# Q and K loaded three tokens to a partition and turned by two identity products of 64 columns, instead of one token to a partition and one transpose of 128 columns

## The chip, the cores and the metric

One core of one Trainium2 chip runs the whole program. A core has a matrix engine (TensorE, PE in the rows, with its weight loads as PEld), a vector engine (DVE), a scalar engine (ACT), GpSimd (POOL) and SyncE (SP), which here issues the DMAs. The metric is the device time of one execution in microseconds (us), smaller is better.

## The reference, cut to what matters

The program chains an attention, a mixture of experts and a gated MLP. Only the first is touched:

```
B, H, S, D = 2, 8, 576, 64
q_d, k_d, v_d = mean of q, k, v over groups of 4 tokens
out_up    = repeat(softmax(q_d k_d^T / 8) v_d, 4)              # coarse, all to all
scores    = q k^T / 8, kept only where |i - j| < 4             # local window
out_local = softmax(scores) v
x = (out_up + out_local) as (1152, 512)
x = sum over 8 experts of P[:, e] * (relu(x @ w1[e]) @ w2[e])  # P from a gate, 8 rounds of scaling
h = x @ w_in;  out = (h * tanh(softplus(h))) @ w_out
```

## The kernel before

The attention works on one pair of heads at a time: 2 batches of 4 pairs give the pairs j = 0 to 7. For every pair Q and K have to lie with the channel on the partition (64 channels of one head above 64 of the other) and the 576 tokens along the free axis, since both score products contract over the channel.

- `load_qk` (tokens LQ and LK of the order) loads one of Q or K of a pair into a tile `qk` of 96 partitions by 12 rows of 64 channels: one DMA for each head, 96 partitions by 6 rows of 64 floats (256 bytes). Token 96u + p lies on partition p. There are 32 such DMAs of 144 KB. All input loads are issued by SP in one queue; four `qk` tiles exist, so a load waits until an older tile has been turned.
- `TP` (TP j.n.i, n = 0 for Q and 1 for K, i for the half of the tokens) turns 288 tokens: three transposes on PE by the identity, each from 96 tokens by 128 channels of both heads to 128 by 96, side by side in one PSUM tile (`at` or `aty`). 32 TPs in all.
- `TQ` and `TK` copy these 288 columns to `qt` or `kt` in SBUF (ACT for most, DVE for some; Q is scaled on the way). After them come `SQ`/`SK` (sums over 4 tokens for the coarse part, mostly POOL), `QL` (L795, the local scores, 16 small products a part, three parts a pair), `QD` (L805, the coarse scores), the softmaxes, `AV` and `AD` (L919, L928, the products with V), `XF` and finally `XH`/`XL` (L948, L951), which write the pair's rows of x as a high and a low half.

The order of all this is written out by hand in a string, ORDER; every engine takes its instructions strictly in that order. Mixed into it are fillers (FL, L1316: products on a constant tile that keep PE occupied), the loads (LD) and scaling of the first expert's weights, and from the token M0.0 on the first expert's products (`G1.products`, L1021), which need x of all four pairs of batch 0. The pairs of batch 1 go on between these products. After the attention PE has the experts' products (L1145, L1176) and then the MLP's.

Of the kernel before, what the change touches and what calls it, by code (L numbers as in the profile page):

```python
# [10 lines left out]
F32 = mybir.dt.float32  # L11
# [10 lines left out]
def attn_moe_moe2_kernel(ctx: ExitStack, tc: tile.TileContext, q, k, v, w_gate, w1, w2, w_in, w_out, out):  # L22
    nc = tc.nc
    B, H, S, D = q.shape
# [17 lines left out]
    QSC = 0.125 / 16.0  # L42
# [524 lines left out]
    ident = const.tile([128, 128], F32, name="ident")  # L567
# [59 lines left out]
    def tensor_engine(eng):  # L627
        return nc.gpsimd if eng == "G" else nc.vector
# [8 lines left out]
    def copy_on(eng, out, in_, scale=None):  # L637
        if eng == "A":
            nc.scalar.activation(out=out, in_=in_, func=AF.Copy, **({} if scale is None else dict(scale=scale)))
        elif scale is None:  # L640
            tensor_engine(eng).tensor_copy(out=out, in_=in_)
        else:
            nc.vector.tensor_scalar(out=out, in0=in_, scalar1=scale, scalar2=None, op0=ALU.mult)
# [5 lines left out]
    class Attention:  # L649
# [4 lines left out]

        def load_qk(self, src, j):

            t = self.p["qk"].tile([96, 12, D], F32, tag="qk", name="qk")
            for h in range(2):
                nc.sync.dma_start(out=t.rearrange("p (u h) d -> p u h d", h=2)[:, :, h],
                                  in_=src[self.b, 2 * j + h].rearrange("(u p) d -> p u d", p=96))  # L660
            return t

        def new_vw(self, j):
# [87 lines left out]
        def TP(self, j, n, i):  # L751

            t = self.st["qk"[n], j]
            ps = at_y() if self.b == 0 and i else self.at()
            for u in range(3):
                nc.tensor.transpose(ps[:, 96 * u:96 * u + 96], t[:, 6 * i + 2 * u:6 * i + 2 * u + 2].rearrange("p u d -> p (u d)"),
                                    ident[0:96, 0:96])
            self.st["T", j, n, i] = ps

        def TQ(self, j, i, eng):  # L760
            copy_on(eng, keep["qt"][j % 2][:, 288 * i:288 + 288 * i], self.st.pop(("T", j, 0, i))[:, 0:288], QSC)

        def TK(self, j, i, eng):
            copy_on(eng, keep["kt"][j % 2][:, 3 + 288 * i:291 + 288 * i], self.st.pop(("T", j, 1, i))[:, 0:288])

        def SQ(self, j, eng):
            self.pool_sum(keep["qd"][j % 2], keep["qt"][j % 2][:, 0:S], eng)
# [526 lines left out]
    with tc.manual_schedule():  # L1294
# [15 lines left out]
        def at_y():  # L1310
            return mm_pools[1][0].tile([128, 512], F32, tag=mm_pools[1][1], name="aty")
# [6 lines left out]
        def at2_tile():  # L1318
            return at2_p.tile([128, 2, 512], F32, tag="att", name="att")

        keep = {n: [pools["keep"].tile(sh, F32, name=f"{n}{i}") for i in range(2)]
                for n, sh in (("qt", [128, S + 8]), ("kt", [128, S + 8]), ("qd", [128, SD]), ("kd", [128, SD]),
                              ("ad", [HM, 2, 2, G, 32]))}
# [57 lines left out]
        def new_h():  # L1381
            return [hp.tile([128, 2, NT], F16, tag="h", name="h") for _ in range(FT)]
# [3 lines left out]
        h = new_h()  # L1386
# [85 lines left out]
        for e in range(1, E):  # L1472
            h = new_h()
# [385 lines left out]
        n = [0]  # L1859
# [27 lines left out]
        for c in range(NC2):  # L1887
            n = [0]
# [49 lines left out]
```

## Time and profile before

| | us |
|---|---|
| median of 3 runs | 968.1 (967.49 to 970.75) |
| the profiled execution, its own time | 969.7 |
| its span, first to last instruction | 967.7 |
| PE busy, share of the span | 949.1, 98% |
| PE products and weight loads | 8504 and 8504 |
| DVE busy | 720.6, 74% |
| ACT busy | 570.5, 59% |
| DMA packets under 512 bytes | 36812 of 97707 |

Busy time says that an engine held an instruction, not that it ran at its peak; neighbouring products overlap in it. The attention of batch 0 fills the first 53 us, that of batch 1 is spread over the next 60 us or so. Matmuls on 32-bit data stand twice in a row's count, a transpose once.

### The profile page before, as it was taken

How to read it: one execution, taken by the hardware profiler on the slowest of the kernel's cores; microseconds unless marked ns; L12 is line 12 of the kernel's file. 1: busy time of each engine (PE TensorE's matmuls, PEld its weight loads, DVE VectorE, ACT ScalarE, POOL GpSimd, SP SyncE). 2: the span in 40 equal slices, each digit the busy share in tenths (PEclk: the TensorE clock that was granted, in tenths of full speed). 3: DMA queues.
4: the chain of work that ended last, by engine and by line, in shares of the span. 5: the costliest groups of instructions: out<-in, count | busy, mean ns of one | idle time of the engine just before them, and what ended most of it. 6: DMA issues, size and time to landing. Idle time of an engine off the chain costs nothing.

```text
span 967.7 us, 20951 instructions
## 1 busy us (share of the span) xinstructions
PE 949.1 (98%) x8504; PEld 651.8 (67%) x8504; DVE 720.6 (74%) x1507; ACT 570.5 (59%) x1162; POOL 62.5 (6%) x116
## 2 busy tenths in 40 slices
PE   5999999999999999999999999999999999999998
PEld 4776674774576467547745764674477577999997
DVE  5887589589678968876796789588766468877731
ACT  4667364675577368646745874685465265666731
POOL 5524200000000000000000000000000000000000
PEclk9999999999999999999999999999999999999999
DMA  9962202021531443063215315141402756766770
GB/s 210 172 150 102 91 11 87 1 80 63 180 131 33 138 152 102 21 208 118 67 60 174 131 39 186 60 143 33 158 1 95 303 191 207 268 208 211 234 271 33
DMA packets 97707, 123.91 MB, mean 128 GB/s; under 512 B 36812, under 2 KB 72012, under 8 KB 96588
## 3 DMA queue, kind: packets, MB, share of 16 engines
q1 hardware_dynamic: 97612, 122.59, 40.4%
q8 instruction: 66, 1.08, 0.5%
q14 instruction: 29, 0.24, 0.1%
HBM read 104.48 MB, written 18.09 MB: 127 GB/s over the span
## 4 chain that ended last, share of the span: by engine, by line
PE 68%; DVE 7%; ACT 2%; DMA 1%; issue 1%; POOL 0%; SPq 0%; ACTq 0%; DVEq 0%; POOLq 0%
PE mm L1145 25%; PE mm L1176 24%; PE mm L1652 9%; PE n L1786 9%; DVE wal L356 1%; DVE acc L1209 1%; DVE raw L360 1%; DVE h L1120 1%; DVE wx L356 1%; DMA raw<-in_moe_w_dram 1%; DVE w L438 1%; DVE w L436 1%; DMA scri<-st 0%; ACT junk L267 0%; DVE st L472 0%
## 5 line engine op out<-in xcount | busy, mean ns | idle before, releaser
L1176 PE MATMUL mm<-wbh,h 128*128 128x512 f16 x1152 | 352.1, 379 | 0.0
L1176 PEld LDWEIGHTS <-h 128*128 128x128 f16 x1728 | 167.8, 98 | 191.9 <-issue 0.4
L1176 PE MATMUL mm<-wbl,h 128*128 128x512 f16 x576 | 218.3, 379 | 0.0
L1145 PE MATMUL mm<-x,wah 128*128 128x288 f16 x672 | 128.2, 286 | 1.5 <-ACT wbh L243 0.8
L1111 DVE SCALAR_TENSOR_TENSOR r<-mm,s 128x288 f32<-128x288 f32 x168 | 76.0, 455 | 71.1 <-PE mm L1145 53.0
L1145 PEld LDWEIGHTS <-wx 128*128 128x128 f16 x1008 | 98.6, 98 | 26.8 <-issue 2.0
L1145 PEld LDWEIGHTS <-wah 128*128 128x128 f16 x896 | 87.7, 98 | 27.8 <-issue 2.0
L1107 ACT ACTIVATE s<-mm 128x288 f32<-128x288 f32 x168 | 66.9, 408 | 58.9 <-PE mm L1145 58.5
L1145 PE MATMUL mm<-xt,wx 128*128 128x288 f16 x672 | 96.4, 286 | 1.3 <-DVE r L1111 1.2
L1652 PEld LDWEIGHTS <-win 128*128 128x128 f16 x1536 | 92.0, 98 | 6.4
L1145 PE MATMUL mm<-x,wal 128*128 128x288 f16 x336 | 96.1, 286 | 0.0
L1120 DVE SCALAR_TENSOR_TENSOR h<-r,h 128x576 f16<-128x576 f32 x112 | 81.2, 750 | 3.0 <-ACT h L1119 3.0
L1119 ACT ACTIVATE h<-r 128x576 f16<-128x576 f32 x112 | 74.1, 676 | 2.1 <-DVE r L1111 2.0
L445 ACT ACTIVATE junk<-w 128x512 bf16<-128x512 f32 x32 | 20.1, 627 | 73.4 <-DVE w L438 66.3
L1659 ACT ACTIVATE s<-mm 128x128 f32<-128x128 f32 x96 | 26.7, 278 | 53.3 <-PE mm L1652 51.4
L1652 PE MATMUL mm<-xc,win 128*128 128x128 f16 x864 | 55.7, 219 | 0.0
L267 ACT ACTIVATE junk<-raw 128x1024 bf16<-128x1024 f32 x52 | 54.6, 1049 | 1.4 <-DMA raw<-in_moe_w_dram 1.0
L98 POOL PARTITION_ALL_REDUCE ma<-m x25 | 12.3, 494 | 648.8 <-DVE m L273 311.5
L1209 DVE SCALAR_TENSOR_TENSOR acc<-mm,pc,acc 128x512 f32<-128x512 f32 x63 | 46.7, 745 | 9.6 <-PE mm L1176 9.6
L1145 PEld LDWEIGHTS <-wal 128*128 128x128 f16 x448 | 43.8, 98 | 11.0
L1145 PE MATMUL mm<-x,wx 128*128 128x288 f16 x336 | 50.3, 286 | 0.0
L1021 PE MATMUL mm<-x,wah 128*128 128x288 f16 x256 | 47.7, 286 | 0.0
(287 smaller groups left out, 1519.6 us busy)
## 6 DMA issues: line engine op xcount, KB each, us to landing
raw<-in_moe_w_dram SPq DMA_DIRECT2D x44, 512.0 KB, 5.4
win<-scri SPq DMA_DIRECT2D x40, 512.0 KB, 5.0
win<-scri SPq DMA_DIRECT2D x40, 384.0 KB, 3.5
raw<-in_moe_w_dram SPq DMA_DIRECT2D x10, 1024.0 KB, 6.2
f<-in_moe_w_in_dram SPq DMA_DIRECT2D x16, 512.0 KB, 3.9
f<-in_moe_w_out_dram SPq DMA_DIRECT2D x16, 512.0 KB, 3.7
scr<-st SPq DMA_DIRECT2D x32, 256.0 KB, 2.3
scri<-st SPq DMA_DIRECT2D x56, 128.0 KB, 1.8
```

The lines of the kernel that those rows point to most:

```text
L267: nc.scalar.activation(out=junk, in_=r[:, c * 1024:(c + 1) * 1024], func=AF.Square, accum_out=mx[:, 2 * i + c:2 * i + c + 1])
L1021: nc.tensor.matmul(self.ps, lhsT=wt[:, ws], rhs=x[:, xi, kk, o:o + CH], start=(n == 0), stop=(n == 3 * KT - 1))
L1107: nc.scalar.activation(out=t, in_=ps, func=AF.Copy, scale=HSC)
L1111: nc.vector.scalar_tensor_tensor(out=out, in0=ps, scalar=HSC, in1=r, op0=ALU.mult, op1=ALU.add)
L1119: lows.append((n + 3, lambda: nc.scalar.activation(out=hi, in_=r, func=AF.Relu)))
L1120: lows.append((n + 6, lambda: nc.vector.scalar_tensor_tensor(out=lo, in0=r, scalar=0.0, in1=hi, op0=ALU.max, op1=ALU.subtract)))
L1145: nc.tensor.matmul(ps, lhsT=w.part(wi, a)[:, c:c + 128], rhs=factor(b, bn, xi, i), start=(not before and k == 0), stop=(k == 5), skip_grou ...
L1176: nc.tensor.matmul(ps, lhsT=h[ft][:, hi, t * 128:(t + 1) * 128], rhs=wt[:, ws], start=(ft == 0 and n == 0), stop=(ft == FT - 1 and n == 2))
L1209: nc.vector.scalar_tensor_tensor(out=a, in0=ps, scalar=pc[:, t:t + 1], in1=a, op0=ALU.mult, op1=ALU.add)
L1652: nc.tensor.matmul(self.bank(bank), lhsT=self.win[i][:, n, wi, kk * 128:(kk + 1) * 128], rhs=self.x[:, xi, xn, kk * 128:(kk + 1) * 128], s ...
L1659: nc.scalar.activation(out=t, in_=self.ps[:, 0], func=AF.Copy)
L1786: nc.tensor.matmul(ps, lhsT=gt(c, f)[:, gi, a, :], rhs=wout[b][:, wi, f, :], start=(k == f == n == 0), stop=(k == len(terms) - 1 and f == ...
```

## The change

Q and K are loaded with three consecutive tokens on a partition: token 288i + 3p + u lies on partition p, so a DMA moves 96 partitions by 2 halves by 192 floats (768 bytes). The tile has the head outside, so the 128 channels of both heads no longer lie side by side; a TP is six products with the identity on the right, 96 tokens by 64 channels each, for u = 0, 1, 2 and for both heads, with the head's half of the PE columns and of the PSUM partitions. PSUM then holds the tokens in the order (u, p), and the copies TQ and TK read it as (p, u), that is with a step of 96 columns, and write `qt` and `kt` in the order of the tokens as before. The line numbers behind the new helper move by 5.

```diff
         def load_qk(self, src, j):
-            t = self.p["qk"].tile([96, 12, D], F32, tag="qk", name="qk")
+            t = self.p["qk"].tile([96, 2, 2, 3 * D], F32, tag="qk", name="qk")
             for h in range(2):
-                nc.sync.dma_start(out=t.rearrange("p (u h) d -> p u h d", h=2)[:, :, h],
-                                  in_=src[self.b, 2 * j + h].rearrange("(u p) d -> p u d", p=96))
+                nc.sync.dma_start(out=t[:, h], in_=src[self.b, 2 * j + h].rearrange("(i p u) d -> p i (u d)", i=2, u=3))
             return t
...
             for u in range(3):
-                nc.tensor.transpose(ps[:, 96 * u:96 * u + 96], t[:, 6 * i + 2 * u:6 * i + 2 * u + 2].rearrange("p u d -> p (u d)"),
-                                    ident[0:96, 0:96])
+                for h in range(2):
+                    nc.tensor.matmul(ps[D * h:D * h + D, 96 * u:96 * u + 96], lhsT=t[:, h, i, D * u:D * u + D],
+                                     rhs=ident[0:96, 0:96], start=True, stop=True, tile_position=(0, D * h))
             self.st["T", j, n, i] = ps
+        def thirds(self, j, n, i, to):
+            copy = self.st.pop(("T", j, n, i))[:, 0:288].rearrange("c (u p) -> c p u", u=3)
+            return to[:, 288 * i:288 * i + 288].rearrange("c (p u) -> c p u", u=3), copy
         def TQ(self, j, i, eng):
-            copy_on(eng, keep["qt"][j % 2][:, 288 * i:288 + 288 * i], self.st.pop(("T", j, 0, i))[:, 0:288], QSC)
+            copy_on(eng, *self.thirds(j, 0, i, keep["qt"][j % 2]), QSC)
         def TK(self, j, i, eng):
-            copy_on(eng, keep["kt"][j % 2][:, 3 + 288 * i:291 + 288 * i], self.st.pop(("T", j, 1, i))[:, 0:288])
+            copy_on(eng, *self.thirds(j, 1, i, keep["kt"][j % 2][:, 3:3 + S]))
```

No instruction changes its place; the rows of every engine stand in the same order as before. On PE, at the start of the program before the change (the TPs of pair 0, then two fillers):

```order
L756 MATMUL at<-ident,qk 128x96 x3
L1316 LDWEIGHTS warm
L1316 MATMUL fill<-warm 128x512
L756 MATMUL aty<-ident,qk 128x96 x6
L756 MATMUL at<-ident,qk 128x96 x3
L1316 LDWEIGHTS warm
```

And the same place of the change:

```order
L756 MATMUL at<-ident,qk 64x96 x6
L1321 LDWEIGHTS warm
L1321 MATMUL fill<-warm 128x512
L756 MATMUL aty<-ident,qk 64x96 x12
L756 MATMUL at<-ident,qk 64x96 x6
L1321 LDWEIGHTS warm
```

Each TP has six products of half the width in the place of three transposes.

## Rows read from the trace of the kernel before

**Rows 1.** Stretches: length, busy time (count) of each engine, clock, DMA share, GB/s.

```profile
12.00:30.00 18.00, 13.88 (x355) 11.25 (x356) 10.01 (x26) 8.40 (x33) 9.84 (x15) 0.91 0.97 199
30.00:53.00 23.00, 21.52 (x613) 16.55 (x612) 21.81 (x46) 18.90 (x48) 12.52 (x14) 1.00 0.98 180
58.00:965.00 907.00, 903.86 (x7393) 616.68 (x7390) 677.49 (x1397) 536.35 (x1063) 33.28 (x46) 1.00 0.37 123
```

**Rows 2.** Waits of PE from 4 to 57 us: total us, times, longest.

```profile
PE att L795 <- issue: 4.1, 2, 2.9
PE mm L1021 <- issue: 1.5, 1, 1.5
PE att L805 <- POOL qd L779: 1.0, 1, 1.0
```

**Rows 3.** Timeline at the first products for x: start us, us.

```profile
52.05 0.81 DVE L951 SCALAR_TENSOR_TENSOR x<-xf,sx,x 128x576 f16<-128x576 f32 x1
...
53.13 0.41 PE L1021 MATMUL mm<-x,wah 128*128 128x288 f16 x2
```

**Rows 4.** Timeline of PE, two TPs early and one between expert products.

```profile
6.34 0.74 PE L756 MATMUL aty<-ident,qk 96*128 96x96 f32 x3 [0.50 <-ACT kt L639]
6.88 0.68 PE L756 MATMUL at<-ident,qk 96*128 96x96 f32 x3
...
57.71 0.41 PE L756 MATMUL at<-ident,qk 96*128 96x96 f32 x3
57.96 0.41 PE L1021 MATMUL mm<-x,wah 128*128 128x288 f16 x2
```

**Rows 5.** AD's four products of 64 columns: timeline, then durations ns min/median/max.

```profile
45.26 0.71 PE L928 MATMUL att<-atd,vd 96*64 96x144 f32 x8
45.90 0.64 PE L727 MATMUL at<-vw,pool_w 128*32 128x128 f32 x12
...
L928 PE MATMUL att<-atd,vd x64: 286/286/338, 34.3 to 109.3; 96*64 96x144 f32 x32, 72*64 72x144 f32 x32
```

**Rows 6.** Stretches between the ends of PE's waits for issue.

```profile
16.35:24.02 7.67, 4.72 (x125) 3.65 (x125) 4.33 (x12) 3.56 (x13) 6.07 (x8) 1.00 0.90 208
24.02:33.60 9.58, 9.21 (x252) 7.67 (x253) 6.91 (x19) 5.75 (x16) 2.68 (x4) 0.82 0.93 174
33.60:44.60 11.00, 10.11 (x253) 7.58 (x252) 10.00 (x24) 9.09 (x26) 9.36 (x11) 1.00 1.10 185
44.60:56.80 12.20, 10.52 (x253) 8.13 (x254) 12.10 (x22) 8.78 (x26) 3.32 (x6) 1.00 0.90 211
```

**Rows 7.** DMA queues: whole run; 16.4 to 21.1 us; 21.1 to 21.3 us.

```profile
q8 instruction: 66, 1.08, 0.5%
...
q1 hardware_dynamic: 2254, 1.33, 117.4%
...
q8 instruction: 1, 0.02, 41.2%
```

**Rows 8.** Two stretches for the DMA rate, then landing of the Q and K loads.

```profile
2.00:8.00 6.00, 3.28 (x15) 2.46 (x16) 4.06 (x18) 1.79 (x5) 1.39 (x25) 1.00 1.21 208
...
56.00:58.00 2.00, 1.14 (x11) 0.99 (x11) 1.43 (x2) 0.09 (x1) 1.58 (x4) 1.00 1.04 355
...
DMA to landing us min/median/max: 2.6/4.2/7.2
```

**Rows 9.** Copies by form: count, busy us, mean ns, idle before.

```profile
L639 ACT ACTIVATE kt<-at 128x288 f32<-128x288 f32 x10 | 4.0, 407 | 0.5 <-PE at L756 0.2
...
L639 ACT ACTIVATE up<-att 128x144 f32<-128x144 f32 x4 | 1.2, 289 | 1.1 <-PE att L928 1.1
...
L811 DVE TENSOR_REDUCE lmx<-att 128x12 f32<-128x384 f32 x8 | 4.4, 544 | 6.5 <-PE att L795 6.5
L855 DVE TENSOR_REDUCE dnm<-att 72x4 f32<-72x576 f32 x8 | 5.9, 733 | 2.2 <-PE att L805 2.2
...
L1252 DVE TENSOR_REDUCE L<-lp 128x72 f32<-128x144 f32 x1 | 0.3, 308 | 1.5 <-PE lp L1244 1.5
```

## The prediction, made before the change was timed

> **What bounds the kernel now.** I read the stretches first, to see in which part of the run the change can matter at all. From 58 us to the end PE is busy for 903.86 of 907 us [rows 1]: whatever delays the experts' products at about 53 us delays the end by as much, and whatever is added to PE behind that point costs its full length. The change touches the attention: 28 of the 32 TPs stand before the first product for the experts (M0.0, at 53.13 us), four between the first products.
>
> So the question is what sets the 53 us. Three engines come into it. DVE is busy for 21.81 of the 23 us from 30 to 53 us, PE for 21.52, and the DMA engines have a mean share of 0.97 and 0.98 from 12 to 53 us [rows 1]. M0.0 starts 0.27 us after the last XL of batch 0 has ended on DVE (52.05 + 0.81) [rows 3]. The waits then tell which of the busy resources is really waited for. Nowhere in the list of PE's waits is there a load of Q or K; those loads land after 7.2 us at most [rows 8]. PE's largest waits, 4.1 us in two pieces and 1.5 us, end by "issue", by nothing that the profile shows [rows 2].
>
> These issue waits have a pattern. Between their ends PE runs 252 + 253 and twice 253 + 252 or 254 products and loads [rows 6], always about 505, and the one before the 24.02 us mark comes after half as many (125 + 125). The whole run has 66 packets on the queue for instructions, 1.08 MB, 16.4 KB each, and PE has 17,008 products and loads (the table above), so about 258 to a packet [rows 7]. I read it so: PE's program is fetched in packets of some 256 instructions, and where the packet is late PE stands still. From 16.4 to 21.1 us the data queue moved 2254 packets at 117% of the engines' share and no instruction packet came; one came between 21.1 and 21.3 [rows 7]; PE went on at 24.02. This idle is also followed by the half clock: the mean granted clock is 0.82 over the next 9.58 us [rows 6], which is 0.18 x 9.58 / 0.5 = 3.4 us at 1.2 GHz, worth 1.7 us.
>
> **The change part by part.**
>
> *Products instead of transposes.* At full clock three transposes take 0.25 us, from 57.71 to 57.96, so 0.083 each; early, at half the pace, 0.54 (6.34 to 6.88) [rows 4]. A product of 96 tokens by 64 columns stands in the trace already: AD's four, with 144 columns to stream, each recorded twice. From the first start to the last end they take 0.71 us, of which the last 0.286; the first is 0.05 longer, so the three steps in between take (0.71 - 0.286 - 0.05) / 3 = 0.125 us [rows 5]. That is three steps for eight records: records go two at a time, one in each half of the columns, and each of the two passes over 144 columns takes one step. For 96 columns a step is 0.125 x 96 / 144 = 0.083, as long as a transpose. The new TP has twelve records in six steps: 0.50 us instead of 0.25. Add the changes between whole-width and half-width work: 0.05 at the entry, and at the exit 45.90 - 45.26 - 0.05 - 4 x 0.125 = 0.09 [rows 5]. A TP beside other split products (L795, L805, L919) had such changes already, so +0.25; one between whole products has them new, twice, so +0.25 to +0.49. I take +0.30 before 53 us, where TPs stand in pairs and beside split work, and +0.45 between the experts' products.
>
> The sum for PE: six TPs at half clock (before 11 us), +0.50 each, 3.0, less the 1.0 that PE waits there for POOL's qd anyway [rows 2], makes 2.0. Nine TPs from 12 to 30 us, 0.30 each, 2.7; in that stretch DVE is busy for only 10.01 of 18 us [rows 1] and waits for PE, so nothing hides it. Thirteen from 30 to 53 us, 3.9; there DVE has nearly no idle time and sets the start of M0.0, and a PE that is a little late is partly hidden: I take half, 2.0 (bounds 0 and 3.9). Four behind M0.0, 1.8, on an engine with no slack. Together 8.5 us (bounds 5.3 and 11.4, with the 1.0 of the wait uncovered).
>
> A page gives a higher price. The Trainium skill, "TensorE: Matmul & The Clock Gate", section Terms, says that the transpose mode is four times as fast for FP32 as an ordinary product; by that a step pair would cost 0.33 us instead of 0.166 and the sum would be about 16 us higher. The rows of AD show two passes, not four, so I keep 0.083.
>
> *Instructions.* A TP had three loads and three products, 6 records; it gets 24. That is 18 x 32 = 576 more, 2.2 packets of 256, nearly all before 75 us. Each can cost between nothing and the longest wait, 2.9 us [rows 2]: 0 to 6.5.
>
> *The loads.* 32 DMAs of 144 KB, 4.7 MB, in pieces of 768 instead of 256 bytes, so a third of the packets. With 256-byte pieces alone the engines moved 208 GB/s (2 to 8 us), with the long rows of the weights 355 [rows 8]. No row has 768; between these ends the 4.7 MB take 22.7 or 13.3 us of the DMA engines' first 57, a relief of 0 to 9.4. Since no Q or K load is waited for, its worth is what the instruction packets gain. All waits that end by issue (4.1 + 1.5) and the half clock (1.7) make 7.3, the most that can come back. I take the 24.02 us wait and its half clock, 2.9 + 1.7 = 4.6, as gone or shortened, and 1.8 for the new packets, since PE now uses a packet up sooner: -2.8 net (bounds -7.3 and +6.5).
>
> *The copies.* 288 columns in groups of three, 96 columns apart. For DVE a row with a step in PSUM exists: L1252 reads 144 elements with a step in 308 ns; the line through 544 ns for 384 and 733 for 576 gives 308 at 144 [rows 9], so the step costs nothing. For ACT there is none with a step at each element; `up`, in runs of 12, lies at 0.82 ns an element below the plain copy. I take 0; if ACT took twice as long for an element, 288 x 0.82 = 0.24 us for each of 28 copies, half of it on the path, 3.4.
>
> *The order* stays, SP's too, so no wait is added for an instruction; the loads are only done earlier.
>
> Sum: 8.5 - 2.8 = +5.7 us. Against the profiled execution's 969.7 that is 975.4; this execution is 1.6 above the median of 968.1, so for the median **973.8**.
>
> **The rivals.**
> 1. The other side: the DMA queue itself, through late instruction packets and the full ring in front of SP, paces everything up to 53 us, and PE's own work is only filling. For it speaks the share of 0.98. Then M0.0 comes up to 9.4 us earlier, the four late TPs cost 1.8: -7.6, 960.5. It decides once the relief passes PE's 8.5. Against it: no load is waited for, and PE is busy for 21.52 of 23 us. The Trainium skill, "DMA: Bandwidth & Descriptors", section Specifications, puts the line rate at transfers of 512 bytes and more, which would put 768 near the upper rate; 208 against 355 GB/s agrees in kind.
> 2. The relief is whole (-7.3) and the new packets cost nothing, so it cancels most of the 8.5: +1.2, 969.3.
> 3. ACT pays for the step in PSUM: +3.4 on top, 977.2.
> 4. The products run one after another, or in four passes as the page says: each TP costs +0.75 and more instead of +0.25, some 16 us on top, 990. AD's rows speak against it.
>
> **How the numbers follow.** Forecast 0.55, rivals 0.08, 0.22, 0.12, 0.03. The forecast's own range, with 30 to 53 us hidden or not and the packets between -4.5 and 0, is 970.5 to 977. To leave out about 2 in 10 I go down to 966, which takes in most of rival 2 but not rival 1, and up to 979.5. A change under 0.3%, 2.9 us, can hardly be told from none in this kernel. Slower (over 971.0): 0.55 x 0.93 + 0.12 + 0.03 = 0.66; same: 0.22 x 0.85 + 0.04 = 0.23; faster: 0.11, rival 1 and the low end of rival 2.
>
> **What would show it.** In the new trace L756 has 384 products, six steps of 0.083 a TP (12 records in about 0.71 us from first start to last end) at full clock. ACT's copies of 128x288 stay at 407 ns. Q and K loads land sooner than the median 4.2 us, and the packets under 512 bytes fall by some 18,000. M0.0 starts at 57 us, give or take 2. The rate of PE's waits for issue tells about the packets: two or three more, none of them near 2.9 us with the half clock behind it. I am wrong if M0.0 comes before 53 us (rival 1), if a TP takes over 1 us (rival 4), or if the copies take 0.6 us (rival 3).

## The result and the profile after

The change makes the kernel slower: 977.2 us median of four executions (974.9 to 979.0) beside 967.8 for the kernel before in the same measurement, a ratio of 1.0089 with a 95% interval of 1.0060 to 1.0118. Five more rounds of the same kernel gave 1.0087 (1.0056 to 1.0118). In microseconds, as (ratio - 1) x 969.5, that is +8.6 (5.8 to 11.4) and +8.4 (5.4 to 11.4); 969.5 is about the median of before in the later rounds, and the same factor is used for every run below. The forecast was 973.8, 5.7 more than before. Two of the eleven executions of one experiment (time_only, its profiled one among them) lay at 987 us, with a mean granted clock of 0.98 where the other nine have 0.996 to 1.000, and are left out of its ratio; of its trace only TPs at full clock are read.

Three stretches of the profile of the change (the first two as in [rows 1]; the third starts later, since the experts' products do), with the columns of [rows 1]:

```profile
12.00:30.00 18.00, 14.19 (x347) 11.00 (x345) 7.30 (x19) 7.34 (x27) 8.15 (x12) 0.81 1.03 221
30.00:53.00 23.00, 22.56 (x615) 17.81 (x607) 18.95 (x48) 16.19 (x44) 14.56 (x15) 1.00 0.52 127
65.00:970.00 905.00, 901.74 (x7377) 614.01 (x7375) 677.14 (x1397) 534.47 (x1060) 32.91 (x46) 1.00 0.37 123
```

From 30 to 53 us PE is now busy for 22.56 of 23 us and DVE for 18.95 instead of 21.81: the engine that had nearly no idle time now waits, and PE is the one without any. Behind 65 us PE is busy to within 3.3 us, much as before (3.1 us of 907 behind 58 us).

The end of the last XL of batch 0 and the first products for the experts (the rows that answer to [rows 3]):

```profile
58.07 0.80 DVE L956 SCALAR_TENSOR_TENSOR x<-xf,sx,x 128x576 f16<-128x576 f32 x1
...
60.22 0.41 PE L1026 MATMUL mm<-x,wah 128*128 128x288 f16 x2
```

M0.0 starts at 60.22 instead of 53.13 us, 7.1 later, and no longer right behind DVE: x is ready at 58.87 and PE comes to M0.0 1.35 us after that. The span is 9.3 longer. So most of the loss lies ahead of M0.0.

PE's waits from 4 to 57 us (those of [rows 2], here from 4 to 60 us): total us, times, longest.

```profile
PE att L810 <- issue: 3.3, 1, 3.3
PE att L800 <- issue: 0.8, 2, 0.5
```

The long wait for issue is still there, and behind as many of PE's products and loads as before (some 690). Two of the others are shorter and the one of 1.5 us at the experts' products is gone; POOL's qd is not waited for any more. Here is the wait, and the clock behind it, in the timeline of PE and in the stretch 22.6 to 29.5 us; the last row is a stretch far behind M0.0.

```profile
23.21 0.87 PE L810 MATMUL att<-kd,qd 64*72 64x144 f32 x5 [3.27 <-issue]
```

```profile
22.60:29.50 6.90, 6.29 (x117) 4.70 (x117) 0.90 (x2) 2.81 (x11) 2.19 (x3) 0.51 0.99 176
124.90:128.60 3.70, 3.70 (x19) 2.39 (x17) 1.35 (x4) 0.41 (x1) 0.00 (x0) 0.54 0.98 372
```

The clock is at 1.2 GHz for nearly all of 6.9 us, and again for 3.4 us at 125 us (0.46 x 3.70 / 0.5), where PE is busy all the time. The kernel before had 3.4 us of it ahead of M0.0 and none at this place. Whether that belongs to the change is a question for the experiments.

The TPs, at half pace (7.21), alone at full clock (42.70 and 43.66) and between the experts' products (76.27):

```profile
7.21 1.23 PE L756 MATMUL aty<-ident,qk 96*64 96x96 f32 x12 [0.51 <-ACT kt L639]
8.22 1.18 PE L756 MATMUL at<-ident,qk 96*64 96x96 f32 x12
...
42.70 0.72 PE L756 MATMUL at<-ident,qk 96*64 96x96 f32 x12
43.34 0.39 PE L1321 MATMUL fill<-warm 128*128 128x512 bf16 x1
...
76.27 0.72 PE L756 MATMUL at<-ident,qk 96*64 96x96 f32 x12
76.91 0.42 PE L1026 MATMUL mm<-x,wah 128*128 128x288 f16 x2
```

A TP takes 0.64 us to the next start at full clock and 1.01 at half pace, where [rows 4] show 0.25 and 0.54. The 0.25 is among the shortest of before; the TP that answers to the one at 76.27 took 0.31:

```profile
69.92 0.47 PE L756 MATMUL at<-ident,qk 96*128 96x96 f32 x3
70.23 0.41 PE L1021 MATMUL mm<-x,wah 128*128 128x288 f16 x2
```

Over the four TPs behind M0.0 the times to the next start sum to 2.58 us, before to 1.15: +0.36 each. Twelve records from first start to last end take 0.72 us, as the prediction said (0.71).

The copies, the packets and the landing of the Q and K loads (by line; the page; by line):

```profile
L639 ACT ACTIVATE kt<-at x12: 402/410/414, 7.0 to 82.4; 128x288 f32<-128x288 f32 x12
```

```profile
DMA packets 85422, 123.96 MB, mean 127 GB/s; under 512 B 18380, under 2 KB 59724, under 8 KB 84300
...
q8 instruction: 69, 1.13, 0.5%
```

```profile
DMA to landing us min/median/max: 2.2/3.4/6.8
```

ACT's copies take 410 ns with the step (407 before). The packets under 512 bytes fall by 18,432, the loads land 0.8 us sooner, and three more instruction packets are fetched. These rows are as the prediction listed them. Two of its signs came out otherwise: M0.0 starts at 60.22, outside 57 give or take 2, and the wait for issue with its half clock stays.

### The profile page after: what moved, and what is told of

The parts are those of the page before. It is cut to its first block, busy times and chain, and to the rows that moved or that the text cites. A ratio compares the mean times of both kernels' runs of the same rounds, so it can differ in the third digit from the quotient of the medians.

```text
span 977.0 us, 21526 instructions
## 1 busy us (share of the span) xinstructions
PE 962.0 (98%) x8792; PEld 661.3 (68%) x8792; DVE 719.8 (74%) x1507; ACT 570.7 (58%) x1162; POOL 62.5 (6%) x116
## 4 chain that ended last, share of the span: by engine, by line
PE 72%; DVE 4%; ACT 1%; DMA 1%; issue 0%; POOL 0%; SPq 0%; ACTq 0%; POOLq 0%
PE mm L1181 29%; PE mm L1150 25%; PE mm L1657 9%; PE n L1791 9%; DMA raw<-in_moe_w_dram 1%; DVE wal L356 0%; DVE h L1125 0%; DVE acc L1214 0%; DVE wx L356 0%; DVE raw L360 0%; DMA scr<-st 0%; ACT junk L267 0%; DVE w L438 0%; DVE w L436 0%; ACT h L1124 0%
```

## The experiments

**The theory** after this trace: the loss is PE's longer work on the 32 TPs; the lighter loads give nothing back, because no load was waited for. **Its rivals:** the lighter loads do give something back, under a larger cost of the products; the strided copies cost; the 576 added instructions cost by themselves; the half clock gets longer. All kernels were timed in five rounds beside the kernel before. The last two columns are of the profiled execution: the start of M0.0, and the time at half clock from 12 to 53 us, worked out from the mean granted clock c of 12 to 30 and of 30 to 53 us as (1 - c) x length / 0.5.

| kernel | ratio (95%) | us | M0.0 | half clock |
|---|---|---|---|---|
| before | 1 | 0 | 53.13 | 3.2 |
| the change | 1.0089 (1.0060 to 1.0118) | +8.6 | 60.22 | 6.8 |
| after_again | 1.0087 (1.0056 to 1.0118) | +8.4 | 55.47 | 0 |
| products_only | 1.0095 (1.0061 to 1.0129) | +9.2 | 61.85 | 10.3 |
| loads_only | 1.0006 (0.9982 to 1.0030) | +0.6 | 51.53 | 6.8 |
| copies_only | 0.9990 (0.9966 to 1.0014) | -1.0 | 50.96 | 6.8 |
| products_15 | 1.0060 (1.0041 to 1.0078) | +5.8 | 59.47 | 10.4 |
| products_13 | 1.0013 (0.9997 to 1.0030) | +1.3 | 59.36 | 10.1 |
| products_4 | 1.0036 (1.0007 to 1.0065) | +3.5 | 52.45 | 6.8 |
| time_only | 1.0043 (1.0029 to 1.0057) | +4.2 | | |
| records_only | 1.0081 (1.0052 to 1.0110) | +7.9 | 55.95 | 0 |
| full_width | 1.0099 (1.0063 to 1.0135) | +9.6 | 57.98 | 0 |
| after_warm | 1.0084 (1.0051 to 1.0117) | +8.1 | 58.65 | 3.2 |
| before_warm | 1.0008 (0.9984 to 1.0031) | +0.8 | 50.79 | 6.8 |

### The change once more

> The changed kernel once more, unchanged. My theory: the time goes into PE's doubled work for each TP (0.64 instead of 0.35 to 0.40 us alone, 1.0 instead of 0.5 at half clock), so the first product for the experts starts again near 60.2 us and the time is 976 to 979 us, 8 to 10 above the kernel before. The half-clock stretch at 125 us, which the first profile of the change had and the one of before had not, I expect to be chance: if it is missing, the span should be some 1.7 us shorter. Rival: the stretch belongs to the change and is there again.

This execution (span 971.1 us) has no half clock at all, neither before M0.0 nor at 125 us:

```profile
12.00:30.00 18.00, 15.31 (x445) 12.19 (x440) 10.28 (x28) 9.62 (x35) 9.64 (x14) 1.00 1.06 206
...
75.00:130.00 55.00, 55.00 (x721) 36.23 (x720) 34.97 (x74) 28.20 (x67) 16.82 (x16) 1.00 0.26 89
```

M0.0 starts at 55.47, not near 60.2: that part of the expectation missed. The stretch at 125 us does not belong to the change: it is missing here, and before_warm (further down), which has the transposes of before, has one of 3.3 us at the same place of the program. It stands behind the 80 products of `lp` there, as in the change and in products_only; the other eleven profiles have these products without it.

```profile
112.50 2.35 PE L1244 MATMUL lp<-wg_hl,x 128*128 128x16 f16 x80
...
115.00:119.00 4.00, 4.00 (x21) 2.65 (x20) 1.32 (x4) 0.41 (x1) 0.00 (x0) 0.59 0.93 345
```

The length of the half clock before M0.0 also differs from execution to execution (6.8 us in the first profile of the change, 0 here). One profile of a kernel says little about either: the six executions of this run lie between 973.1 and 980.1 us.

### The three parts apart

products_only, in `load_qk` (the head outside; pieces of 256 bytes and the order of the tokens as before) and `TP`:

```diff
-            t = self.p["qk"].tile([96, 12, D], F32, tag="qk", name="qk")
+            t = self.p["qk"].tile([96, 2, 6, D], F32, tag="qk", name="qk")
...
+                nc.sync.dma_start(out=t[:, h],
...
+                for h in range(2):
+                    nc.tensor.matmul(ps[D * h:D * h + D, 96 * u:96 * u + 96], lhsT=t[:, h, 3 * i + u],
+                                     rhs=ident[0:96, 0:96], start=True, stop=True, tile_position=(0, D * h))
```

> The kernel before with the six products of 64 columns alone: the loads keep their 256-byte pieces and the order of the tokens, the copies stay plain. My theory (all the time is PE's, the loads bring nothing): 976 to 979 us, as the whole change, and the first product for the experts near 60 us. Rival, the lighter loads do give back the 2.8 us that I predicted, hidden under a larger cost of the products: then this kernel is slower than the whole change, 979.5 to 981. Rival, the strided copies or the new loads cost part of the 9 us: then this one is 971 to 974.

loads_only, with `load_qk` as in the change, in `TP`:

```diff
-                nc.tensor.transpose(ps[:, 96 * u:96 * u + 96], t[:, 6 * i + 2 * u:6 * i + 2 * u + 2].rearrange("p u d -> p (u d)"),
-                                    ident[0:96, 0:96])
+                nc.tensor.transpose(ps[:, 96 * u:96 * u + 96], t[:, u % 2, i, u // 2 * D:u // 2 * D + 2 * D], ident[0:96, 0:96])
```

> The kernel before with the loads of 768-byte pieces alone: each TP is three transposes of 128 columns as before, taken from 128 neighbouring columns of the new tile, and the copies are plain. The tokens and heads come out mixed up (the output is another one), the work is the same. My theory: no load is waited for, so the time stays within 2 us of before, 966 to 970, and the wait for instructions before the third hundred of PE records stays near 3 us. Rival, relief as I predicted: 965.0 or less (2.8 us and more gained), with that wait shortened. Rival, the new loads cost: 970.5 and more.

copies_only, in `TQ`, and in the same way in `TK`, with the change's `thirds`:

```diff
-            copy_on(eng, keep["qt"][j % 2][:, 288 * i:288 + 288 * i], self.st.pop(("T", j, 0, i))[:, 0:288], QSC)
+            copy_on(eng, *self.thirds(j, 0, i, keep["qt"][j % 2]), QSC)
```

> The kernel before with the strided copies alone: the loads and transposes as before, so the copies put the tokens of each half into another order (the output is another one). My theory: a copy of 128 by 288 takes ACT 410 ns with or without the step, so the time stays within 2 us of before, 966 to 970. Rival (the third of the prediction): the step costs, 3.4 us or more on top, 971.5 and up, with copies of over 0.5 us.

The products alone cost +9.2 (5.9 to 12.5), as much as the whole. The loads alone give +0.6 (-1.7 to +2.9), the copies alone -1.0 (-3.3 to +1.4). So the products are the whole loss as far as these intervals tell, and the interval of the loads does not reach the gain of 2.8 that the prediction took. The row of the copies:

```profile
L639 ACT ACTIVATE kt<-at x12: 391/408/412, 6.1 to 72.4; 128x288 f32<-128x288 f32 x12
```

In loads_only the landing and the waits of PE are as follows:

```profile
DMA to landing us min/median/max: 2.4/3.6/7.0
```

```profile
PE att L803 <- POOL qd L777: 2.7, 2, 2.3
PE att L793 <- issue: 1.2, 2, 0.6
```

Here the long wait for issue is indeed gone, against my expectation that it would stay. But the half clock is not: from 13 to 22 us the granted clock has a mean of 0.62, behind the wait for qd. In copies_only, where no load is changed, the long wait is gone too (its waits for issue at the local scores sum to 1.1 us in three), and it too has 6.8 us at half clock. With either kind of load the wait and the half clock are long in one profile and short in another.

```profile
13.00:22.00 9.00, 8.45 (x158) 6.65 (x161) 5.28 (x15) 3.44 (x14) 5.13 (x9) 0.62 1.05 242
```

### The products by stages

products_15, in `TP`, with the loads and copies as before; products_13 and products_4 have the condition for their TPs:

```diff
             for u in range(3):
+                if NP * self.b + j + (1 - n) / 2 + i / 4 < 3.75:
+                    for h in range(2):
+                        nc.tensor.matmul(ps[D * h:D * h + D, 96 * u:96 * u + 96], lhsT=t[:, 6 * i + 2 * u + h],
+                                         rhs=ident[0:96, 0:96], start=True, stop=True, tile_position=(0, D * h))
+                    continue
```

> The kernel before, with the six products only in the first fifteen TPs (pair 0 to TP3.0.0, before about 30 us). The prediction gave these 2.0 + 2.7 us. Theory A, only PE's time counts: +4 to +5, 973 to 974. Theory B, the later PE also meets a longer stretch at half clock, as in the trace of the change (0.81 from 12 to 30 us): 975 to 977, and the profile shows a mean granted clock from 12 to 30 us below the 0.91 of before.

> The kernel before, with the six products of 64 columns only in the thirteen TPs that stand between about 30 and 53 us (TP3.0.1 to TP6.0.0); loads and copies as before. The prediction gave these 2.0 us (half of 3.9 hidden behind DVE). My theory after the trace of the change: next to nothing is hidden, +3.9 us, 972 to 974. Rival, hidden as predicted or better: 971 or less.

> The kernel before with the six products only in the four TPs of pair 7, behind the first product for the experts; loads and copies as before. The prediction gave these 4 x 0.45 = 1.8 us, with nothing to hide them: 971.0 to 972.5 beside a kernel before of 969.5. Rival, hidden there too: 970.3 or less. Together with the first fifteen (+5.7) and the thirteen (+0.9) this should make the 8.8 of the whole if nothing but these sums is at work.

The first fifteen cost +5.8 (4.0 to 7.6), the thirteen +1.3 (-0.3 to +2.9), the last four +3.5 (0.7 to 6.3). The thirteen in the stretch where DVE has no idle time are hidden for at least a quarter when they stand alone, since the 3.9 of the theory is outside the interval: that part of it falls. That they looked exposed in the first profile of the change because PE was already late there, with DVE no longer setting the pace (18.95 us busy), is a reading of that trace; no run isolates it. For the first fifteen, 975.7 us and a clock of 0.80 from 12 to 30 us are what theory B named (975 to 977, below 0.91), but the mean granted clock of all six executions is 0.995 and that of before in the same rounds 0.996, and +5.8 has theory A's 4 to 5 inside its interval: A and B are not told apart. The parts add up to 10.6 where the whole is 8.6; with such intervals that is no contradiction. The profiles of products_15 and products_13 have some 10 us at half clock each, and the times of their M0.0 are read with that in mind:

```profile
22.00:33.00 11.00, 8.89 (x168) 7.24 (x168) 2.64 (x5) 3.97 (x14) 4.02 (x5) 0.54 0.95 175
```

```profile
36.00:48.00 12.00, 11.66 (x198) 9.12 (x198) 4.29 (x9) 5.12 (x16) 6.38 (x8) 0.57 0.90 180
```

The first of these is products_15, the second products_13; the execution of products_13 that was profiled took 973.9 us, 3 us more than the median of its kernel (970.9).

### PE's time or the number of instructions

time_only, ahead of the three transposes of `TP`:

```diff
+            nc.tensor.matmul(ps[:, 288:440], lhsT=ident[0:96, :], rhs=t.rearrange("p u d -> p (u d)")[:, 0:152], start=True, stop=True)
```

records_only, at the same place:

```diff
+            for _ in range(9):
+                nc.tensor.matmul(ps[:, 288:289], lhsT=warm[:, 0:128], rhs=warm[:, 0:1], start=True, stop=True)
```

full_width, in the place of the transposes:

```diff
-                nc.tensor.transpose(ps[:, 96 * u:96 * u + 96], t[:, 6 * i + 2 * u:6 * i + 2 * u + 2].rearrange("p u d -> p (u d)"),
-                                    ident[0:96, 0:96])
+                nc.tensor.matmul(ps[:, 96 * u:96 * u + 96], lhsT=t[:, 6 * i + 2 * u:6 * i + 2 * u + 2].rearrange("p u d -> p (u d)"),
+                                 rhs=ident[0:96, 0:96], start=True, stop=True)
```

> The kernel before, with one FP32 product of 152 columns ahead of each TP's three transposes, into columns of the PSUM tile that nobody reads: some 0.25 us of PE per TP, as the change adds, in few instructions (4 records per TP against the 18 that the change adds). My theory, PE's time is the cost and not the number of instructions: 975 to 979 us. Rival, the added instructions (2.2 more packets of 256) are what costs: 968 to 972 us.

> The kernel before, with nine products of one column ahead of each TP's transposes: 18 records per TP, as many as the change adds, and by an estimate from the weight loads' durations some 0.23 us of PE. My theory: as time_only, within 2 us, 975 to 979. Rival, instructions cost by themselves: 3 us or more above time_only.

> The kernel before with each transpose of 128 columns written as an ordinary FP32 product of 128 columns with the identity: by the two passes seen in AD's rows the same six steps of 0.083 us per TP as the change, but 12 records instead of 24 (6 before), and no change between whole and half width. Theory A, PE's time costs: 975 to 979 us, little below the products alone. Theory B, which time_only and records_only speak for (+4.5 with 4 more records of 0.30 us, +7.9 with 18 more of 0.24 us a TP): the number of instructions costs some 3 us of the 9, and this kernel gains them back: 973 to 975. If an FP32 product took four passes, a TP would take 1.0 us and the kernel 983 or more.

The timeline of PE at one TP at full clock: time_only, records_only, full_width (there one of its shortest).

```profile
30.82 0.53 PE L755 MATMUL at<-qk,ident 96*128 96x152 f32 x2
31.18 0.41 PE L757 MATMUL at<-ident,qk 96*128 96x96 f32 x3
```

```profile
30.49 0.38 PE L756 MATMUL at<-warm 128*128 128x1 bf16 x9
30.73 0.45 PE L758 MATMUL at<-ident,qk 96*128 96x96 f32 x3
```

```profile
60.92 0.81 PE L756 MATMUL at<-ident,qk 96*128 96x96 f32 x6
61.56 0.41 PE L1021 MATMUL mm<-x,wah 128*128 128x288 f16 x2
```

What is added to a TP's PE time is 0.36 us here in time_only, 0.24 in records_only and 0.64 - 0.25 = 0.39 in full_width, with 4, 18 and 6 more records; the cost is +4.2 (2.8 to 5.5), +7.9 (5.0 to 10.7) and +9.6 (6.1 to 13.1). Over the four TPs behind M0.0, all at full clock, the times to the next start sum to 2.26, 2.15 and 2.80 us, in the change to 2.58 and in before to 1.15, so +0.28, +0.25, +0.41 and +0.36 each. A step of full_width takes 0.107 to 0.12 us by this and not the 0.083 of its expectation: the products of 64 columns, side by side in pairs, come out a little cheaper here (2.58 against 2.80 us).

Added PE time costs in all three; but neither measure alone puts them in order. By time, time_only should lie beside records_only, and lies 3.7 below, as the rival in the expectation of records_only had it; by the number of instructions, full_width should lie beside time_only, and lies 5 above. The trace of full_width has no wait for issue between 12 and 62 us and a granted clock of 1.00 from 12 to 53 us, so what it lost there (M0.0 at 57.98) is PE's time; the trace of records_only has waits for issue of at most 0.54 us each. That speaks for time.

Part of the disorder is the clock. The mean granted clock of the executions in the ratio is 0.998 in time_only, 0.995 in records_only and 0.999 in full_width, and 0.996 in before. Over the 69 executions of before in these rounds a mean clock lower by 0.01 goes with 5.1 us more. Set right by that (an estimate), the three cost some 5, 7 and 11 us, and the change, whose clock is that of before, its 8.5. Time_only is then 2 us below records_only and no longer 4; what is left is not explained, and a share of the instructions in the 8.6 us is not excluded.

### A warmer start

before_warm and after_warm, at the start of ORDER (FL5:G is two products on the constant tile):

```diff
-        "LK0 TP0.1.0 LQ0 FL5:V LK1 TP0.1.1
+        "FL5:G FL5:G FL5:G LK0 TP0.1.0 LQ0 FL5:V LK1 TP0.1.1
```

> The kernel before with the same six products ahead of its first TP. If PE is then at full pace, the first six TPs cost 0.35 to 0.40 instead of 0.5 to 0.6 each, of which some goes into the wait for POOL's qd: 1 to 1.5 us faster, 968 to 968.5 beside a kernel before of 969.5, which may be too little to tell. Rival: nothing is gained, or the half clock comes at another place and costs as much.

> The changed kernel with six products on the constant tile (512 columns each) ahead of the first TP, in time in which PE otherwise waits for the first load. If PE is then at full pace for the first six TPs, each costs 0.64 or less instead of 1.0 to 1.1, and the chain before 12 us is up to 2 to 3 us shorter: 975 us. Rival: the start is paced by the first loads, the copies and POOL, or the pace does not rise: 977 to 978, as the change.

Neither gains: +0.8 (-1.6 to +3.0) against before, and +8.1 for the change with it beside +8.4 without. In before_warm the TPs do come to full pace earlier, but the wait for POOL's qd takes all of it. Its timeline of PE (two TPs that before took 0.54 and 0.48, then the coarse scores, which before started at 12.06 after a wait of 1.02):

```profile
6.42 0.47 PE L756 MATMUL aty<-ident,qk 96*128 96x96 f32 x3 [0.50 <-ACT kt L639]
6.73 0.41 PE L756 MATMUL at<-ident,qk 96*128 96x96 f32 x3
6.97 0.60 PE L1316 MATMUL fill<-warm 128*128 128x512 bf16 x2
...
12.00 0.34 PE L805 MATMUL att<-kd,qd 64*72 64x144 f32 x1 [2.56 <-POOL qd L779]
```

In after_warm the pace of the TPs stays at half up to 10 us in spite of the same six products:

```profile
7.84 1.23 PE L756 MATMUL aty<-ident,qk 96*64 96x96 f32 x12 [0.51 <-ACT kt L639]
8.85 1.18 PE L756 MATMUL at<-ident,qk 96*64 96x96 f32 x12
```

So that PE waits for POOL there, and what this wait can hide, is shown; no version was found that beats the kernel before.

## Why the prediction was right, and some 3 us low

**What held.** The kernel is slower, by a mechanism that the prediction named. The measured 977.2 us lies inside 966 to 979.5 and just above the forecast's own 970.5 to 977 (by its terms, 6.5 to 10.4 for the products and -4.5 to 0 for the packets, that range would be 970.1 to 978.5). The price of a TP was right: six steps, two passes, halves of the columns side by side, 0.64 us instead of 0.25. So was the sum for the products, 8.5 us, against +9.2 (5.9 to 12.5) for the products alone and +8.6 for the whole. That it came so close is in part luck: the TPs were priced a little high, and less of their time was hidden than the 3 us taken off. Before anything is hidden they came to 11.4 us; the timelines give 9.9, with +0.42 for each of the first six and +0.36 for each of the last four in the change, and +0.27 for each of the 22 between in after_again. By its terms:

- The first fifteen TPs: 2.0 + 2.7 = 4.7 predicted, +5.8 (4.0 to 7.6) measured. The 1.0 us of the wait for POOL's qd was rightly taken as cover: in the change there is no such wait, and the coarse scores start at 13.19 instead of 12.06, 1.1 us later.
- The thirteen: 2.0, half hidden behind DVE; +1.3 (-0.3 to +2.9).
- The four behind M0.0: 1.8; +3.5 (0.7 to 6.3). In the timeline of the change they add 2.58 - 1.15 = 1.4, which the interval includes.
- The copies: 0; -1.0 (-3.3 to +1.4), 410 ns.

**The step that failed** is the term for the instructions and the loads together: "I take the 24.02 us wait and its half clock, 2.9 + 1.7 = 4.6, as gone or shortened, and 1.8 for the new packets, since PE now uses a packet up sooner: -2.8 net". In place of -2.8 the loads alone gave +0.6 (-1.7 to +2.9), and the whole lies 8.6 - 5.7 = 2.9 above the forecast, which is this term. The loads became lighter just as said (a third of the packets, landing 0.8 us sooner), but the wait that they were to shorten is not a fixed property of the kernel. The longest wait for issue ahead of M0.0 was 2.9 us in the profile of before, and in others with its loads 4.1 (products_15), 2.0 (products_4), 0.5 (copies_only) and none from 12 us on (full_width); with the new loads it was 3.3 (the change), 2.1 (after_again), 3.0 (after_warm) and 0.6 (loads_only). The half clock wanders likewise, from 0 to 10 us before M0.0. Five profiles with the transposes of before up to M0.0 (before, loads_only, copies_only, products_4, before_warm) have a mean of 6.1 us of it and M0.0 at 51.8 us; four with all products changed (the change, after_again, products_only, after_warm) 5.1 us and 59.0. So the half clock is not longer in the change; the clocks of all executions say the same, 0.9957 in the mean of ten of the change and 0.9958 in that of 69 of before. M0.0 is 7.3 us later on average. With the four late TPs (1.4 by the timeline) that makes 8.7, near the measured 8.6. I had read one execution's wait as something that a change could give back.

**The rivals.** M0.0 later, not earlier, than before rules out the first (paced by the DMA queue; whether a full ring holds SP back, no row shows by itself); the loads alone the second (whole relief); 410 ns and copies_only the third. The fourth (serial products or four passes) is ruled out by 0.64 us a TP. The Trainium skill, "TensorE: Matmul & The Clock Gate", section Terms, puts the transpose mode at four times the speed of an FP32 product. Here full_width compares just these, the same 128 columns by transpose and by product: 0.25 and 0.64 us at the shortest, 2.6 times, and 1.15 and 2.80 us over the four TPs behind M0.0, 2.4 times.

**What stays open:** how much of the 8.6 us, if any, the added instructions cost beside PE's time (time_only is 4 us cheaper than records_only and the change, some 2 to 3 by the estimate from the clocks), and what decides in which execution the wait for issue and the half clock come where.

## What to carry to other kernels

Ask of a lighter transfer first whether anything waits for it: here 18,432 fewer small packets were worth nothing that could be measured, while 0.25 to 0.5 us more per TP on the engine without slack, some 10 us in all, cost 8.6. A wait "for issue" or a stretch at half clock seen in one profile is one draw; before a change is credited with removing it, look for it in a second execution. Where two engines share a stretch as its bound (PE and DVE from 30 to 53 us), a small delay of one is partly hidden (the thirteen TPs there cost +1.3 alone); that a larger delay uncovers it is how the traces read, and no run shows it by itself.

## What the runs showed of the hardware that was not expected

- Six products on a constant tile ahead of the first TP (1.3 to 4.4 us) brought the TPs to full pace by 6.7 us in before_warm, but not by 9 us in after_warm. In both stretches the profile's row for the granted clock says 1.00 (as it does for 0 to 12 us of the kernel before, where TPs also took twice as long): in the first 12 us the pace has to be read from durations.
- The half clock also comes while PE is busy all the time (3.70 of 3.70 us from 124.9 to 128.6 in the change, 4.00 of 4.00 from 115 to 119 in before_warm). In the three profiles that have it there it follows the 80 products of 16 columns that take 2.35 us; in the other eleven the same products are not followed by it.
- A full-width FP32 product with 96 columns to stream needs 0.64 / 6 = 0.107 us a record at the shortest and 0.12 in the mean of the four TPs behind M0.0 (2.80 / 24), the half-width ones 0.053 (0.64 / 12), two of them side by side.
